# First MLP, blocks 8 to 17: normalisation and transposed parts issued ahead of the weight conversion steps

## The chip, the cores and the metric

The kernel runs on one core of a Trainium2 chip. The metric is the device time in microseconds of one execution. The kernel before was run three times: median 850.16 us, 850.09 to 852.99.

## The reference, cut to what matters

2304 tokens (4 batches of 576) of width 512 pass through three layers:

```python
x = attention(q, k, v, M_prev, z_prev, beta)   # 8 heads of 64, causal, with a memory term
h = x @ w_in                                   # first MLP, 512 -> 1024
e = exp(h - max(h)); solu = h * e / sum(e)
ln = (solu - mean(solu)) / sqrt(var(solu) + 1e-6) * g_ln
x = ln @ w_out                                 # 1024 -> 512
gate = sigmoid(x @ w_gate)                     # second MLP, 512 -> 1536
out = (gate * (x @ w_val)) @ w_out2            # 1536 -> 512
```

All weights come from DRAM as 64-bit floats.

## The kernel before, in words

**Layout.** The tokens are 18 blocks of 128 rows (t = 0 to 17). `X` stays on chip and holds the activations transposed. The attention runs first (lines up to 600), then the first MLP (`Moe1`), then the second (`Moe2`). The first MLP's blocks 0 to 7 overlap with the end of the attention and with the conversion of the first MLP's own weights; the change concerns the loop in `Moe1.run` over t = 8 to 17 and the entry into it, the branch for t = 8 (`t == NF1`). T1 is block 7. In the profiled execution the entry lies at about 266 us, the second MLP begins at about 431 us.

**One block of the first MLP.** Every product is done in three terms, since each operand is split into a high and a low part. The steps of block t, with their engines and lines:

- `h` (L658, TensorE): 48 matmuls into the PSUM tile `h`, which has two buffers.
- `max` (L671, VectorE), `exp` (L676, ACT, into the tile `e`), `mul` (L680 to L682, VectorE), `square` (L687 on ACT, then three tiny operations on GpSimd, L688 to L691, that yield scale and bias of the normalisation), `norm` (L695, ACT, in place on `e`).
- `trans` (L705, TensorE): eight transposes of `e` into two PSUM tiles `pl`, four each. There are two `pl` buffers in all, so the next block's transposes can write them only when this block's have been read by `parts(t, 0)` (L713, ACT: high parts into `lnT`) and by `parts(t, 1)` (L715, VectorE: low parts).
- three blocks form a group, and `product` (L724, TensorE) multiplies a group's `lnT` by the second weights into the PSUM tiles `po` (two buffers; po_0 to po_3 are the four column blocks of the result). `result` (L734, ACT) copies a finished `po` into `X`. `pieces(t)` hands out a group's products in halves, three halves for each block.
- `xsplit` (L644 ACT, L646 VectorE or GpSimd) splits the input of block t + 2 into the tile `xs`.

`ahead(t, n)` issues the first half of block t's `h` matmuls, then the transposes of block n, then the second half. So TensorE, which runs its instructions in order, waits in the middle of `h(t)` whenever the transposes of block t - 2 can't start.

**Weight conversion.** Beside this the loop converts the weights of the second MLP for its first six chunks (`Moe2.convert`, f = 0 to 5; `EARLY` is 6; the other six chunks are converted within the second MLP). A chunk is 15 steps: five each for w_val, w_gate and w_out. Of five steps, the first takes the exponent (L108, VectorE) and shifts it (L118, ACT), the second takes the mantissa (L111, VectorE), the third the sign (L121, VectorE, needs L118), the fourth the low word (L125, VectorE), and the fifth multiplies (L947, GpSimd). Among them stand sums of weight parts (L961, GpSimd, on the tile `M`), high parts `hi` (L969, ACT) and low parts `lo` (L975, VectorE, in place on `M`; for some parts GpSimd), and for w_out `hi_o` (L988, ACT, into the tile `ho`) and `lo_o` (L994, GpSimd). SP's queue saves the results to DRAM (L981, L982, L997) and loads the next raw weights (L105, into two buffers `raw`). Six end steps of a chunk are merged into the first six steps of the next chunk:

```python
chunk[4].append(loads[n][2])            # w_out of this chunk
chunk[9].append(loads[n + 1][0])        # w_val of the next
chunk[14].append(loads[n + 1][1])       # w_gate of the next
for x, y in zip(chunk, ends[n - 1]):
    x += y
```

**What sets the order.** Every engine runs its instructions in the order in which the program issues them, so the order in which `run` calls these functions is the schedule. `go(n)` issues the next n conversion steps. For t = 9 to 16 the order is: go(3); ahead(t, t - 2); high parts of t - 2; norm(t - 1); max(t); exp(t); go(2); low parts of t - 2; xsplit, mul(t), xsplit; square(t); three times a piece of products and go(1); then the steps left for this block. By the end of blocks 8 to 17 there are 24, 33, 41, 50, 58, 67, 75, 84, 93 and 96 steps issued.

## Time and profile before

| | |
|---|---|
| median of 3 runs | 850.16 us |
| profiled execution | 850.23 us, of which the span of the trace 848.4 us |
| mean granted TensorE clock | 0.994 |
| TensorE matmul (PE) busy | 831.8 us, 98% |
| TensorE weight load (PEld) busy | 734.2 us, 87% |
| VectorE (DVE) busy | 630.5 us, 74% |
| ACT busy | 467.9 us, 55% |
| GpSimd (POOL) busy | 481.0 us, 57% |

A share is busy time over the span, averaged over stages with different limits. A busy TensorE is not one at full speed: the granted clock tells that. The timeline shows one engine's instructions by start and duration, and behind a row the time for which the engine had stood idle and the instruction that released it. What an idle stretch costs is read from the engine that sets the pace of its stage.

### The profile page before, as it was taken

How to read it: one execution, taken by the hardware profiler on the slowest of the kernel's cores; microseconds unless marked ns; L12 is line 12 of the kernel's file. 1: busy time of each engine (PE TensorE's matmuls, PEld its weight loads, DVE VectorE, ACT ScalarE, POOL GpSimd, SP SyncE). 2: the span in 40 equal slices, each digit the busy share in tenths (PEclk: the TensorE clock that was granted, in tenths of full speed). 3: DMA queues.
4: the chain of work that ended last, by engine and by line, in shares of the span. 5: the costliest groups of instructions: out<-in, count | busy, mean ns of one | idle time of the engine just before them, and what ended most of it. 6: DMA issues, size and time to landing. Idle time of an engine off the chain costs nothing.

```text
span 848.4 us, 14831 instructions
## 1 busy us (share of the span) xinstructions
PE 831.8 (98%) x5020; PEld 734.2 (87%) x5020; DVE 630.5 (74%) x1379; ACT 467.9 (55%) x995; POOL 481.0 (57%) x579
## 2 busy tenths in 40 slices
PE   7999999999999999899999999999999999999998
PEld 5777777777788989799999999899999999999996
DVE  6899999997898687796447778878766445746645
ACT  5899999996697466676433345344533223424221
POOL 4787778774565667685406856876555242442111
PEclk9899999999999999999999999999999999999999
DMA  6544444430222455563278849993998773391662
GB/s 135 128 104 98 123 103 115 102 89 21 84 78 76 137 194 173 188 195 126 81 287 323 251 182 322 405 330 114 328 406 291 249 217 93 119 379 37 248 235 100
DMA packets 134971, 154.08 MB, mean 182 GB/s; under 512 B 69744, under 2 KB 103792, under 8 KB 134896
## 3 DMA queue, kind: packets, MB, share of 16 engines
q1 hardware_dynamic: 134576, 153.07, 55.5%
q8 instruction: 40, 0.66, 0.3%
q14 instruction: 35, 0.29, 0.1%
q10 hardware_dynamic: 320, 0.07, 0.0%
HBM read 116.92 MB, written 36.18 MB: 180 GB/s over the span
## 4 chain that ended last, share of the span: by engine, by line
PE 75%; DVE 9%; ACT 5%; DMA 4%; POOL 4%; issue 2%; SPq 0%; ACTq 0%; POOLq 0%; DVEq 0%
PE s L1114 16%; PE acc L1167 16%; PE g L1114 8%; PE po L724 7%; PE x L492 5%; PE sc L383 4%; PE v L1114 4%; PE h L658 3%; PE x L477 2%; PE sc L374 2%; DVE e L682 1%; PE trf L293 1%; DVE consts L671 1%; PE trk L293 1%; DMA raw<-in_moe_w_val_dram 1%
## 5 line engine op out<-in xcount | busy, mean ns | idle before, releaser
L1167 PE MATMUL acc<-o,G 128*128 128x512 f32 x648 | 181.6, 390 | 0.2 <-DVE G L1133 0.2
L1152 POOL TENSOR_TENSOR vl<-vl,sg 128x384 f32<-128x384 f32 x36 | 37.0, 1028 | 206.2 <-ACT sg L1151 206.2
L1167 PEld LDWEIGHTS acc<-o,G 128*128 128x128 f32 x648 | 118.6, 188 | 10.2 <-DVE G L1133 0.7
L422 POOL TENSOR_SCALAR p<-p,first,cols 128x256 f32<-128x256 f32 (+3 forms) x142 | 97.8, 703 | 6.3 <-DVE first L416 4.3
L411 ACT ACTIVATE p<-p,nm 128x128 f32<-128x128 f32 (+2 forms) x144 | 83.7, 595 | 2.0 <-DVE nm L405 0.8
L658 PE MATMUL h<-wih,xs 128*128 128x512 f32 x288 | 84.7, 400 | 0.0
L1144 ACT ACTIVATE sg<-sg 128x384 f32<-128x384 f32 x36 | 18.9, 526 | 104.1 <-DVE sg L1143 104.0
L724 PE MATMUL po<-lnT,woh 128*128 128x384 f32 x288 | 73.3, 335 | 0.0
L1133 DVE TENSOR_TENSOR G<-vl,G 128x384 fp32r<-128x384 f32 x72 | 54.4, 756 | 21.4 <-ACT G L1130 21.3
L1130 ACT CAST G<-vl 128x384 fp32r<-128x384 f32 x72 | 37.1, 515 | 45.2 <-POOL vl L1152 36.4
L658 PEld LDWEIGHTS h<-wih,xs 128*128 128x128 f32 x288 | 52.7, 190 | 10.5 <-POOL xs L646 0.7
L1151 ACT ACTIVATE sg<-sg 128x384 f32<-128x384 f32 x36 | 19.0, 526 | 75.2 <-DVE sg L1150 75.1
L405 DVE CUSTOM_DVE_ANT_0 p<-sc,mask 128x128 f32<-128x128 f32 (+3 forms) x128 | 54.9, 484 | 2.4 <-PE sc L383 1.4
L118 ACT ACTIVATE ex<-ex,consts 128x512 int32<-128x512 int32 (+1 forms) x52 | 34.7, 667 | 34.0 <-DVE ex L108 34.0
L724 PEld LDWEIGHTS po<-lnT,woh 128*128 128x128 f32 x288 | 52.0, 188 | 0.3
L947 POOL TENSOR_TENSOR M<-ex 128x256 f32<-128x256 f32 x48 | 42.6, 908 | 13.8 <-DVE ex L125 13.8
L724 PE MATMUL po<-lnT,wol 128*128 128x384 f32 x144 | 48.2, 335 | 0.0
L1138 DVE TENSOR_TENSOR u<-s,p 128x384 f32<-128x384 f32 x36 | 20.0, 556 | 36.0 <-PE s L1114 35.9
L333 POOL TENSOR_TENSOR G<-E,zm 128x640 f32<-128x640 f32 x16 | 25.0, 1563 | 37.7 <-DVE E L330 32.5
L121 DVE SCALAR_TENSOR_TENSOR ex<-raw,ex 128x512 int32<-128x512 int32 (+1 forms) x52 | 39.9, 767 | 7.7 <-ACT ex L118 7.6
L658 PE MATMUL h<-wil,xs 128*128 128x512 f32 x144 | 45.1, 394 | 0.0
L961 POOL TENSOR_TENSOR M<-M 128x256 f32<-128x256 f32 x48 | 42.2, 889 | 1.3
(710 smaller groups left out, 2442.6 us busy)
## 6 DMA issues: line engine op xcount, KB each, us to landing
o<-scro SPq DMA_DIRECT2D x36, 512.0 KB, 4.3
scrg<-hi SPq DMA_DIRECT2D x36, 256.0 KB, 4.6
scrg<-M SPq DMA_DIRECT2D x36, 256.0 KB, 4.6
raw<-in_moe_w_val_dram SPq DMA_DIRECT2D x12, 512.0 KB, 5.8
raw<-in_moe_w_gate_dram SPq DMA_DIRECT2D x12, 512.0 KB, 4.4
raw<-in_moe_w_out_dram SPq DMA_DIRECT2D x12, 512.0 KB, 5.1
scro<-ho SPq DMA_DIRECT2D x12, 512.0 KB, 2.8
out_dram<-X SPq DMA_DIRECT2D x18, 256.0 KB, 2.0
```

Source lines behind the costliest of these rows:

```text
L121: nc.vector.scalar_tensor_tensor(ex, raw[:, :, 1], -0x80000000, ex, ALU.bitwise_and, ALU.bitwise_or)
L405: nc.vector.tensor_tensor_reduce(p, x, m, -1.0, 3.0e38, ALU.add, ALU.min, nm)
L411: nc.scalar.activation(p, p, AF.Exp, bias=nm, scale=-1.0, accum_out=self.sum[n % 2][:, c, 0:1])
L422: eng.tensor_scalar(p, p, r["rs"][:, c : c + 1], og, ALU.mult, ALU.mult)
L492: nc.tensor.matmul(r["x", g][64 * hh : 64 * hh + 64, c0 : c0 + src.shape[1]], r["vt"][:, c : c + D], src, start=False, stop=j == 0,)
L658: lambda s=s, w=w, j=j: nc.tensor.matmul(ph[:, j * 512 : j * 512 + 512], xs[:, s, c], self.wi[c][w][:, j * 512 : j * 512 + 512], start=(c ...
L724: nc.tensor.matmul(self.po[g, m], w[:, m * P : m * P + P], L[x][c // 4][:, c % 4], start=(c == 0 and n == 0), stop=(c == NF1 - 1 and n == 2),)
L947: nc.gpsimd.tensor_mul(out[:, sl], m[:, sl], e[:, sl])
L961: ops[i][0](*ops[i][1:])
L1114: nc.tensor.matmul(po, W[:, a, c * P : c * P + P], xb[b][:, c], start=c + i == 0, stop=c == 1 and i == 2)
L1133: nc.vector.tensor_sub(G[:, 1, hs[h]], vl[:, h], f32(G[:, 0, hs[h]]))
L1167: nc.tensor.matmul(po, G[:, x, sl], o[:, w], start=first and i == 0, stop=stop and i == 2)
```

## The change

The body of the loop becomes a list of letters, `STEADY`, that is read for t = 8 to 17: m is `max`, e `exp`, g with a number so many conversion steps and g alone all that are left for this block, r the low parts of t - 2, x0 and x1 the two halves of `xsplit`, u `mul`, s `square`, p the next piece of products, n `norm(t)`, a `ahead(t + 1, t - 1)`, and q0 the high parts of t - 1. So `norm(t)` stands behind the pieces of block t, where before it stood in block t + 1 behind `go(3)` and the high parts; the transposes of t - 1 and their high parts follow within block t, ahead of the rest of its conversion steps; and the `go(3)` ahead of every block's maximum is gone. The steps that stood there come later, so that fewer steps have been issued when a block's maximum comes (58 and not 61 before that of block 13), but as many by the end of a block.

In the branch for t = 8, products and copies of block 7's pieces come first, with no step between the first two pieces, and `norm(T1)` follows the third; the transposes and both parts of block 6 follow at once.

In `convert`, for the six chunks of the first MLP, `lo(0, 2)` moves from the chunk's last step to the second end step, two steps later, and the two DMAs of `save(0, 2)` from the first end step to the third, behind `save_o`. The second MLP's own conversion (f from 6) keeps the old places.

```diff
@@ -25,6 +25,9 @@
 g1_c:0 n23_r:0 lz:2 s2_m:1 s3_p:1 g0_p:0 ph_s:1 s1_e:1 g0_c:0 s3_m:1 tt_p:0 n3_p:0 n2_p:0 cv_d:1 tf_p:1 t3_p:0
 tt_c:0 n01_r:1 cv_h:0 tc_p:0 tc_c:0 cv_l:0 tf_c:1 s4_p:1 t0_p:0 s4_m:1 ph_e:2
 """.split()
+
+
+STEADY = "m e g2 r x0 u x1 s g1 p g1 p g1 p n g1 a q0 g"


 COPY = dict(tc="v", tt="s", kh="s", x0="v", x1="v", g0="s", g1="v", t0="s", t1="s", t2="s", t3="s")
@@ -827,34 +830,46 @@
                 later += conv[done:n]
                 done = n
                 if t == NF1:
-                    go(3)
-                    self.norm(T1)
-                    for f, copy in self.pieces(T1):
+                    for i, (f, copy) in enumerate(self.pieces(T1)):
                         f(), copy and copy()
-                        go(2)
+                        if i == 2:
+                            self.norm(T1)
+                        go(0 if i == 0 else 3)
                     for x in range(2):
                         self.trans(t - 2, x)
-                else:
-                    if t < NBLK - 1:
-                        go(3)
-                    ahead(t, t - 2)
-                self.parts(t - 2, 0)
-                if t > NF1:
-                    self.norm(t - 1)
-                self.max(t)
-                self.exp(t)
-                go(2 if t < NBLK - 1 else 0)
-                self.parts(t - 2, 1)
-                if t + 2 < NBLK:
-                    self.xsplit(t + 2, 0)
-                self.mul(t)
-                if t + 2 < NBLK:
-                    self.xsplit(t + 2, 1)
-                self.square(t)
-                for f, copy in self.pieces(t):
-                    f(), copy and copy()
-                    go(1)
-                go(len(later))
+                    for x in range(2):
+                        self.parts(t - 2, x)
+                    assert t == NF1
+                todo = self.pieces(t)
+                for x in STEADY.split():
+                    if x[0] == "g":
+                        go(int(x[1:]) if x[1:] else len(later))
+                    elif x == "p":
+                        for f, copy in todo[:1]:
+                            f(), copy and copy()
+                        del todo[:1]
+                    elif x in ("x0", "x1"):
+                        if t + 2 < NBLK:
+                            self.xsplit(t + 2, int(x[1]))
+                    elif x == "m":
+                        self.max(t)
+                    elif x == "e":
+                        self.exp(t)
+                    elif x == "u":
+                        self.mul(t)
+                    elif x == "s":
+                        self.square(t)
+                    elif x == "r":
+                        if t > NF1:
+                            self.parts(t - 2, 1)
+                    elif t + 1 == NBLK:
+                        pass
+                    elif x == "n":
+                        self.norm(t)
+                    elif x == "a":
+                        ahead(t + 1, t - 1)
+                    else:
+                        self.parts(t - 1, int(x[1]))

         def pieces(self, t):

@@ -1007,10 +1022,12 @@
                 [v[0]], [v[1]], [v[2]], [v[3]], [new_m, v[4]],
                 [g[0]], [g[1], lambda: sums(0)], [g[2]], [g[3]], [g[4]],
                 [o[0], lambda: sums(1, 2)], [o[1], lambda: sums(3)], [o[2], lambda: hi(0, 2)], [o[3], lambda: hi(2, 4)],
-                [lambda: lo(0, 2), o[4], lambda: hi(4, 6)],
+                [*([] if f < EARLY else [lambda: lo(0, 2)]), o[4], lambda: hi(4, 6)],
             ]
             return loads, steps, [
-                [lambda: hi(6, 7), hi_o, lambda: save(0, 2)], [lo_o], [lambda: lo(4, 6, nc.gpsimd), save_o],
+                [lambda: hi(6, 7), hi_o, *([] if f < EARLY else [lambda: save(0, 2)])],
+                [lo_o, *([lambda: lo(0, 2)] if f < EARLY else [])],
+                [lambda: lo(4, 6, nc.gpsimd), save_o, *([lambda: save(0, 2)] if f < EARLY else [])],
                 [lambda: lo(6, 7, nc.gpsimd), lambda: save(4, 6)], [lambda: lo(2, 4), lambda: save(6, 7)], [lambda: save(2, 4)],
             ]
```

The order of TensorE's instructions is the same in both kernels. That of VectorE, ACT and GpSimd changes, and SP's in six places, one for each chunk. In the following rows a name with a number is a tile and its instance; line numbers of the changed kernel are higher by 3, behind `run` by 15.

**ACT, block 8 (the branch for t = 8).** `h_4012<-e_4111` is the square of block 7, `e_4111<-e_4111` its normalisation, `X<-po_...` the copies of the first three results, `ex` a conversion step. Before:

```order
L687 ACTIVATE h_4012,consts<-e_4111,consts 128x1024
L118 ACTIVATE ex_4146<-ex_4146,consts 128x512
L695 ACTIVATE e_4111<-e_4111,consts 128x1024
L734 COPY X<-po_0_3904 128x6x64
L734 COPY X<-po_1_3905 128x6x64
L118 ACTIVATE ex_4166<-ex_4166,consts 128x512
L734 COPY X<-po_2_4169 128x6x64
```

Now:

```order
L690 ACTIVATE h_4012,consts<-e_4111,consts 128x1024
L737 COPY X<-po_0_3904 128x6x64
L737 COPY X<-po_1_3905 128x6x64
L121 ACTIVATE ex_4154<-ex_4154,consts 128x512
L698 ACTIVATE e_4111<-e_4111,consts 128x1024
L737 COPY X<-po_2_4158 128x6x64
```

The copies of po_0 and po_1 stand directly behind the square; a conversion step and the normalisation come behind them.

**ACT, from the square of block 12 to its normalisation.** `h_4728<-e_4767` (now `h_4704<-e_4752`) is the square, `e_4767<-e_4767` (now `e_4752<-e_4752`) the normalisation of block 12, `lnT<-pl` the high parts of block 11, `hi`, `ho` and `ex` are conversion. Before:

```order
L687 ACTIVATE h_4728,consts<-e_4767,consts 128x1024
L734 COPY X<-po_1_4696 128x6x64
L118 ACTIVATE ex_4813<-ex_4813,consts 128x512
L734 COPY X<-po_2_4800 128x6x64
L969 CAST hi_4834<-M_4713 128x512 x3
L118 ACTIVATE ex_4844<-ex_4844,consts 128x512
L969 CAST hi_4834<-M_4713 128x256
L988 CAST ho_4848<-ex_4813 128x512
L713 CAST lnT_4608<-pl_0_4865 128x4x128
L713 CAST lnT_4608<-pl_1_4870 128x4x128
L695 ACTIVATE e_4767<-e_4767,consts 128x1024
```

Now:

```order
L690 ACTIVATE h_4704,consts<-e_4752,consts 128x1024
L737 COPY X<-po_1_4686 128x6x64
L737 COPY X<-po_2_4795 128x6x64
L698 ACTIVATE e_4752<-e_4752,consts 128x1024
L716 CAST lnT_4592<-pl_0_4840 128x4x128
L716 CAST lnT_4592<-pl_1_4845 128x4x128
L121 ACTIVATE ex_4864<-ex_4864,consts 128x512
L984 CAST hi_4872<-M_4754 128x512
L679 ACTIVATE e_4875,consts<-h_4827,consts 128x1024
```

The normalisation follows the copy of po_2, and behind it the high parts of block 11; the conversion instructions that stood between come elsewhere.

**VectorE, the same place.** `xs` is the input of block 14, `consts<-h` the maximum of block 13, `lnT<-pl` the low parts of block 11, `M<-M,hi` the low part of a weight, the other rows are conversion steps. Before:

```order
L646 TENSOR_TENSOR xs_4773<-X,xs_4773 128x2x4x64
L108 TENSOR_SCALAR ex_4813<-raw_4716 128x512
L111 TENSOR_SCALAR ex_4813<-raw_4716 128x512
L121 SCALAR_TENSOR_TENSOR ex_4813<-raw_4716,ex_4813 128x512
L125 SCALAR_TENSOR_TENSOR ex_4813<-raw_4716,ex_4813 128x512
L975 TENSOR_TENSOR M_4713<-M_4713,hi_4834 128x512
L108 TENSOR_SCALAR ex_4844<-raw_4798 128x512
L671 TENSOR_REDUCE consts<-h_4852 128x1
L111 TENSOR_SCALAR ex_4844<-raw_4798 128x512
L121 SCALAR_TENSOR_TENSOR ex_4844<-raw_4798,ex_4844 128x512
L715 TENSOR_TENSOR lnT_4608<-pl_0_4865,lnT_4608 128x4x128
L715 TENSOR_TENSOR lnT_4608<-pl_1_4870,lnT_4608 128x4x128
```

Now:

```order
L649 TENSOR_TENSOR xs_4769<-X,xs_4769 128x2x4x64
L114 TENSOR_SCALAR ex_4762<-raw_4665 128x512
L124 SCALAR_TENSOR_TENSOR ex_4762<-raw_4665,ex_4762 128x512
L128 SCALAR_TENSOR_TENSOR ex_4762<-raw_4665,ex_4762 128x512
L111 TENSOR_SCALAR ex_4864<-raw_4757 128x512
L114 TENSOR_SCALAR ex_4864<-raw_4757 128x512
L124 SCALAR_TENSOR_TENSOR ex_4864<-raw_4757,ex_4864 128x512
L674 TENSOR_REDUCE consts<-h_4827 128x1
L128 SCALAR_TENSOR_TENSOR ex_4864<-raw_4757,ex_4864 128x512
L718 TENSOR_TENSOR lnT_4592<-pl_0_4840,lnT_4592 128x4x128
L718 TENSOR_TENSOR lnT_4592<-pl_1_4845,lnT_4592 128x4x128
```

`M<-M,hi` no longer stands there, and one L108 less; one L125 (now L128) more stands behind the maximum.

**SP, the saves of chunk 0.** `scrg` and `scro` are the DRAM copies of the parts, `raw` the loads. Before:

```order
L105 DMA raw_4261<-in_moe_w_gate_dram 128x4x256
L981 DMA scrg_3602<-hi_4237 128x2x256
L982 DMA scrg_3602<-M_4161 128x2x256
L997 DMA scro_3603<-ho_4267 128x1024
L981 DMA scrg_3602<-hi_4237 128x2x256
L982 DMA scrg_3602<-M_4161 128x2x256
L105 DMA raw_4336<-in_moe_w_out_dram 128x1024
```

Now:

```order
L108 DMA raw_4262<-in_moe_w_gate_dram 128x4x256
L1012 DMA scro_3603<-ho_4268 128x1024
L996 DMA scrg_3602<-hi_4237 128x2x256
L997 DMA scrg_3602<-M_4174 128x2x256
L996 DMA scrg_3602<-hi_4237 128x2x256
L997 DMA scrg_3602<-M_4174 128x2x256
L108 DMA raw_4337<-in_moe_w_out_dram 128x1024
```

The two saves of `save(0, 2)` stand behind that of `ho` and no longer ahead of it; the two of `save(4, 6)` and the w_out load follow as before.

## Rows read from the trace of the kernel before

**Rows 1.** The page, part 1: busy us, share of the span, instructions.

```profile
PE 831.8 (98%) x5020; PEld 734.2 (87%) x5020; DVE 630.5 (74%) x1379; ACT 467.9 (55%) x995; POOL 481.0 (57%) x579
```

**Rows 2.** Windows: bounds, length, busy us (count) of each engine, PEclk, DMA share, GB/s.

```profile
431.00:848.40 417.40, 412.46 (x2161) 383.69 (x2159) 275.90 (x451) 145.77 (x273) 193.38 (x194) 1.00 0.71 248
...
272.00:431.00 159.00, 154.24 (x841) 143.70 (x842) 110.00 (x169) 91.95 (x160) 97.88 (x128) 0.99 0.47 153
```

**Rows 3.** Timeline of PE: start, duration, instruction, [idle before <-releaser], three marked gaps.

```profile
272.82 1.33 PE L724 MATMUL po<-lnT,wo 128*128 128x384 f32 x6 [1.45 <-ACT X L734]
...
315.38 1.22 PE L705 MATMUL pl<-ident,e 128*128 128x128 f32 x8 [0.85 <-DVE lnT L715]
...
354.68 1.97 PE L705 MATMUL pl<-ident,e 128*128 128x128 f32 x8 [3.08 <-ACT e L695]
```

**Rows 4.** Timeline of PE: first halves of blocks 11 to 15.

```profile
311.60 0.63 PE L658 MATMUL h<-wih,xs 128*128 128x512 f32 x2
...
325.46 0.63 PE L658 MATMUL h<-wih,xs 128*128 128x512 f32 x2
...
338.11 0.63 PE L658 MATMUL h<-wih,xs 128*128 128x512 f32 x2
...
348.68 0.63 PE L658 MATMUL h<-wih,xs 128*128 128x512 f32 x2
...
366.25 0.63 PE L658 MATMUL h<-wih,xs 128*128 128x512 f32 x2
```

**Rows 5.** Windows: two microseconds behind the stall of block 12.

```profile
356.00:358.00 2.00, 2.00 (x8) 1.71 (x7) 1.97 (x5) 0.76 (x2) 0.00 (x0) 0.50 0.85 289
```

**Rows 6.** Timeline of ACT: block 8, normalisation and copies to X.

```profile
271.16 1.24 ACT L695 ACTIVATE e<-e,consts 128x1024 f32<-128x1024 f32 x1 [0.82 <-POOL consts L691]
272.31 0.84 ACT L734 COPY X<-po 128x384 f32<-128x384 f32 x2
```

**Rows 7.** Timeline of ACT: high parts of block 11, normalisation of block 12.

```profile
352.42 1.07 ACT L713 CAST lnT<-pl 128x512 fp32r<-128x512 f32 x2
353.38 1.25 ACT L695 ACTIVATE e<-e,consts 128x1024 f32<-128x1024 f32 x1
```

**Rows 8.** Timeline of POOL: last number for the normalisation of block 12.

```profile
344.97 0.77 POOL L691 TENSOR_SCALAR consts<-consts 128x1 f32<-128x1 f32 x1
```

**Rows 9.** Timeline of DVE: from xs of block 14 to lnT of block 11.

```profile
342.59 0.69 DVE L646 TENSOR_TENSOR xs<-X,xs 128x512 fp32r<-128x512 f32 x1
...
344.98 0.71 DVE L121 SCALAR_TENSOR_TENSOR ex<-raw,ex 128x512 int32<-128x512 int32 x1 [1.02 <-ACT ex L118]
...
349.00 0.69 DVE L975 TENSOR_TENSOR M<-M,hi 128x512 fp32r<-128x512 f32 x1 [2.71 <-POOL M L961]
...
350.50 1.21 DVE L671 TENSOR_REDUCE consts<-h 128x1 f32<-128x1024 f32 x1
...
353.04 1.29 DVE L715 TENSOR_TENSOR lnT<-pl,lnT 128x512 fp32r<-128x512 f32 x2 [0.29 <-ACT lnT L713]
```

**Rows 10.** All instructions on tile raw, 255 to 440 us: ns min/median/max, starts.

```profile
L108 DVE TENSOR_SCALAR ex<-raw x18: 414/476/968, 269.1 to 383.6; 128x512 int32<-128x512 int32 x18
L111 DVE TENSOR_SCALAR ex<-raw x18: 415/472/964, 269.4 to 384.3; 128x512 int32<-128x512 int32 x18
L121 DVE SCALAR_TENSOR_TENSOR ex<-raw,ex x18: 679/709/1174, 270.4 to 386.6; 128x512 int32<-128x512 int32 x18
L125 DVE SCALAR_TENSOR_TENSOR ex<-raw,ex x18: 676/684/1228, 271.0 to 387.2; 128x512 f32<-128x512 uint16 x18
```

**Rows 11.** Timeline of DVE: first w_out step ahead of block 9's maximum; lnT of block 8.

```profile
299.14 0.75 DVE L108 TENSOR_SCALAR ex<-raw 128x512 int32<-128x512 int32 x1 [3.03 <-DMA raw<-in_moe_w_out_dram]
...
314.56 1.27 DVE L715 TENSOR_TENSOR lnT<-pl,lnT 128x512 fp32r<-128x512 f32 x2
```

**Rows 12.** Timeline of SP: a save of chunk 0 and the w_out load behind it.

```profile
293.57 0.36 SPq L982 DMA_DIRECT2D scrg<-M  x1
294.02 0.45 SPq L105 DMA_DIRECT2D raw<-in_moe_w_out_dram  x1
```

## The prediction

> **What bounds the kernel now.** I read the busy shares first: TensorE is busy 98% of the span [rows 1]. So only its gaps, and time that it spends at a slow clock, can be won, and the windows say where they lie: from 272 to 431 us, where most of the change works, TensorE is busy 154.24 of 159 us; behind 431 us, in the second MLP, 412.46 of 417.4 [rows 2]. The order there is untouched, so what the first MLP gains should be handed on nearly whole.
>
> TensorE's timeline has three marked gaps in the stretch [rows 3]. po_2, a product of block 8, waits 1.45 us for ACT's copy of po_0 into X, until 272.82. The transposes of block 9 wait 0.85 us for a low part on VectorE, until 315.38. Those of block 12 wait 3.08 us, put down to ACT's normalisation, until 354.68.
>
> A gap is not the whole price. The first halves of blocks 11 to 15 start at the times in [rows 4]: 12 to 13 takes 12.65 us without a stall. 11 to 12 and 14 to 15 hold the same work, but take 13.86 and 17.57. So the wait of 0.85 us costs 13.86 - 12.65 = 1.21 us, and that of 3.08 us costs 17.57 - 12.65 = 4.92. The extra 1.8 us of the latter is the clock: the granted share is 0.50 in 356 to 358 us, the 1.2 GHz level, after TensorE had done nothing from 351.60 to 354.68 [rows 3, 5]. In all 1.45 + 1.21 + 4.92 = 7.58 us can be won here.
>
> **The change part by part.** No instruction is added or removed. TensorE's order stays; those of ACT, VectorE and GpSimd change, and six places of SP's queue.
>
> *Block 8 (the T1 branch).* Before, ACT runs a conversion step behind the square, waits 0.82 us for GpSimd's scale, normalises block 7 (271.16), and only then copies po_0 and po_1 out (272.31) [rows 6]. Now the copies stand right behind the square. What ends last is then po_0 itself, complete at the latest when TensorE stopped, at 272.82 - 1.45 = 271.37. One copy is half of 0.84 us: po_2 can start by 271.8, which wins 1.0 us; if po_0 was complete sooner (three products of po_1 stand behind it), up to 1.45. I take **-1.2 us**, near the middle. The normalisation comes later by two copies; nothing reads it before the transposes of block 7, which stand behind all of block 8's products.
>
> *Transposes of block 12.* Two locks hold them, not one. The timeline names the normalisation, but the transposes also write the two pl tiles that block 11's transposes filled, and these come free when VectorE has read them: its lnT pair starts at 353.04 and takes 1.29, to 354.33, only 0.35 us before the transposes [rows 3, 9].
>
> The first lock: GpSimd's last number for this normalisation was ready at 344.97 + 0.77 = 345.74 [rows 8]. ACT got to it at 353.38, behind six conversion instructions and the high parts [rows 7]. Now it follows the copy of po_2 directly: it can run from 345.8 to 347.0, over 4 us before TensorE wants it at 351.60.
>
> The second: behind the normalisation come the high parts of block 11 at once (1.07 us, so to 348.1; they stood at 352.42) [rows 7]. On VectorE the low part of the weights, which waited 2.71 us for GpSimd (it overwrites in place what GpSimd's sums still read), no longer stands ahead of the maximum [rows 9]. From the end of xs (342.59 + 0.69 = 343.28) up to lnT there are now two each of L111, L121 and L125, one L108 and the maximum. With the medians of [rows 10] and 1.21 for the maximum that is 5.42 us, with the 1.02 us wait for ACT that [rows 9] shows 6.4: lnT starts at 349.7 and frees the first pl at 350.4. With every one at its longest it is 8.9 + 1.0: the first pl is free at 353.8. TensorE wants it at 351.60, so between 0 and 2.2 us of the stall stay. I take 0.2, since the medians are likelier than seven longest ones in a row: **-4.7 us**.
>
> *Transposes of block 9.* lnT of block 8 began at 314.56. Between xs of block 9 and it VectorE has ten instructions before and ten after, of like durations, so this stretch doesn't shrink by itself. What shrinks is its start: the maximum of block 9 stood behind the first step on the w_out weights, which waited 3.03 us for its load until 299.14 [rows 11]. Now that step comes behind the maximum and behind lnT of block 7. The chain ends up to 3 us earlier, where 0.85 was short: **-1.2 us**. The bounds are 0 (the wait only moves behind lnT) and 1.21.
>
> *The low part and the saves of each chunk.* One VectorE subtraction goes two steps back in the list, its duration stays. With it two saves move behind the save of ho, and so come directly ahead of GpSimd's saves and the next chunk's w_out load in SP's queue. Issues follow each other there at 0.45 us (293.57, 294.02) [rows 12], so five loads may leave 2 x 0.45 = 0.9 us later. It is hidden by the maximum (1.21) and lnT (1.28), which now run ahead of the step that needs the load; without that cover it costs up to 0.9 us in each of five chunks.
>
> *The rest.* As many steps as leave the place ahead of the maximum now run elsewhere. In blocks 14 to 16 that may leave a low part late: by the smallest such wait in the trace 1.21 us, by blocks without one nothing. I put 0.5 in between.
>
> Sum: -1.2 - 4.7 - 1.2 + 0.5 = -6.6 us. The profiled execution took 850.23 us (span 848.4), the median is 850.16, so nothing is to be corrected: **843.6 us**.
>
> **A rule that speaks against it.** The w_out load was issued at 294.02, behind the saves, and VectorE stood until 299.14 for it [rows 11, 12]. The Trainium skill's page "DMA: Bandwidth & Descriptors", section "Rules for kernel authors", says to issue a DMA early and to wait for its semaphore late; by it a change that puts saves ahead of a load loses. The trace agrees with it at that load. What its mechanism would cost here is rival 2.
>
> **The rivals.**
> 1. *The second lock stays shut*, or the stall only moves. ACT's steps for VectorE now queue behind the normalisation and the high parts; if VectorE waits there for them, lnT is as late as before. Then the big stall gives only the 0.35 us between the locks: 850.2 - 1.2 - 1.2 - 0.35 = 847.5 us, and with block 9 unmended too 848.7. For it: VectorE's total work doesn't shrink, and its idle time is waits for others [rows 9, 11]. Against it: the longest of those, 2.71 and 3.03 us, are just the ones that move. In this case the change doesn't do what it says.
> 2. *Slower: the w_out load becomes the bound.* If GpSimd's low parts still come late, the load leaves 0.9 us later, while VectorE asks for it no later, and waits 3.03 + 0.9 us; the next maximum and lnT queue behind that. It decides when this is more than VectorE's lead at the next transposes; each then costs TensorE a stall like the one of 3.08 us, 4.92 with the clock. In three of five chunks: 850.2 - 7.1 + 14.8 = 857.9 us. For it: the load was late once already. Against it: that wait of 3.03 us cost TensorE 1.21 at most.
> 3. *No wait at all is left*: 850.2 - 7.58 = 842.6 us.
>
> **How the numbers follow.** Forecast, with rival 3 in it (842.4 to 845.9): 0.70. Rival 1 (846 to 850): 0.22. Rival 2: 0.08. A measurement of this kernel can tell about 0.5% from no change, 4.25 us, so faster means under 845.9 and slower over 854.4: 0.70, 0.22 and 0.08. The range is 842.4 to 848.4: below it nothing is left to win here, and above it I leave out rival 2 and the tail of rival 1. What the second lock may keep (2.0 us over the sum, 845.6) and the uncovered loads (5 x 0.9 = 4.5 over it, 848.1) lie inside.
>
> **What would show it.** Right: from block 8's products to the second MLP no wait of TensorE over 1 us for a normalisation or a copy, no granted share below 1, the copies of po_0 and po_1 ahead of the normalisation, and the second MLP starting some 6.6 us sooner and taking as long as before. Wrong: the transposes wait for lnT instead of e; VectorE waits over 3 us for w_out loads in several chunks; the second MLP takes longer by what the first one gave.

## The result and the profile after

The changed kernel takes 843.59 us, median of 4 runs (843.14 to 844.54); the kernel before 850.74 beside it. The ratio is 0.9913, interval 0.9891 to 0.9934. Timed again in a later series, it gave 0.9925 (0.9906 to 0.9944). The profiled execution took 843.14 us.

The page, its span and part 1, against [rows 1], and the windows from 272 us to the first product of the second MLP and behind it, against [rows 2]:

```profile
span 841.3 us, 14834 instructions
...
PE 827.1 (98%) x5020; PEld 730.4 (87%) x5020; DVE 626.8 (74%) x1379; ACT 469.3 (56%) x995; POOL 482.7 (57%) x579
```

```profile
272.00:423.25 151.25, 150.47 (x832) 140.54 (x831) 108.09 (x171) 92.27 (x158) 98.98 (x128) 1.00 0.48 161
423.25:841.30 418.05, 412.38 (x2161) 383.81 (x2160) 274.67 (x451) 145.95 (x273) 194.07 (x194) 1.00 0.70 248
```

TensorE is now busy 150.47 of 151.25 us in the first window. The granted clock there is 1.00.

TensorE's timeline of the kernel before at three marks (the start of block 8's `h`, the transposes of block 6, which stand behind block 7's products, and the first product of the second MLP):

```profile
256.25 0.63 PE L658 MATMUL h<-wih,xs 128*128 128x512 f32 x2
...
281.28 1.03 PE L705 MATMUL pl<-ident,e 128*128 128x128 f32 x8
...
430.91 0.33 PE L1114 MATMUL g<-xb11h,gv0g 128*128 128x384 f32 x1
```

The same marks after, with the transposes that answer to [rows 3], and the first halves of blocks 14 and 15 that answer to [rows 4]:

```profile
255.03 0.63 PE L661 MATMUL h<-wih,xs 128*128 128x512 f32 x2
...
278.65 1.03 PE L708 MATMUL pl<-ident,e 128*128 128x128 f32 x8
...
312.68 1.23 PE L708 MATMUL pl<-ident,e 128*128 128x128 f32 x8 [0.78 <-DVE lnT L718]
...
345.95 0.63 PE L661 MATMUL h<-wih,xs 128*128 128x512 f32 x2
...
348.72 1.03 PE L708 MATMUL pl<-ident,e 128*128 128x128 f32 x8
...
358.59 0.63 PE L661 MATMUL h<-wih,xs 128*128 128x512 f32 x2
...
423.25 0.33 PE L1131 MATMUL g<-xb11h,gv0g 128*128 128x384 f32 x1
...
436.10 0.45 PE L1131 MATMUL g<-xb21h,gv1g 128*128 128x384 f32 x1 [1.17 <-DVE u L1155]
```

The wait of po_2 is gone, that of block 12's transposes too (348.72, no bracket, 1.03 us and not 1.97). That of block 9's transposes is still there, 0.78 us. A longer wait stands in the second MLP, 1.17 us at a product of its second chunk (`g<-xb21h,gv1g`) where before there were 0.27. It is the eleventh product there; the expectations below count wrongly and call it the sixth.

The difference of the marks from kernel to kernel tells where the 7.1 us of the two spans (848.4 - 841.3) come from:

| stretch | before - after at its end | gained in it |
|---|---|---|
| attention, to block 8 | 256.25 - 255.03 = 1.22 | 1.22 |
| block 8 | 281.28 - 278.65 = 2.63 | 1.41 |
| to block 14, with block 9's transposes | 348.68 - 345.95 = 2.73 | 0.10 |
| block 14, with block 12's transposes | 366.25 - 358.59 = 7.66 | 4.93 |
| to the second MLP | 430.91 - 423.25 = 7.66 | 0.00 |
| second MLP | 848.4 - 841.3 = 7.1 | -0.56 |

The 1.22 us of the attention aren't the change's. In the fourteen profiles of this text, all with the same attention, block 8 starts between 254.68 and 257.09 us. The second MLP, where its order is the same, takes 417.2 to 419.7 us. So spans are compared below by **the first MLP's stretch**, from the first product of block 8 to the first of the second MLP: 430.91 - 256.25 = 174.66 us before, 423.25 - 255.03 = 168.22 after, and 168.22 again in the repetition. That is 6.44 us less. Each stretch is read from one profile; where the first MLP is the same it repeats closely: 168.22 twice for the change, 167.08 to 167.10 in e7, e9 and e12.

ACT after, answering to [rows 6] and [rows 7], and VectorE ahead of the transposes of blocks 9 and 12 (there from xs of block 14), answering to [rows 11] and [rows 9]:

```profile
269.67 1.00 ACT L737 COPY X<-po 128x384 f32<-128x384 f32 x2 [1.59 <-PE po L727]
...
271.19 1.24 ACT L698 ACTIVATE e<-e,consts 128x1024 f32<-128x1024 f32 x1
...
339.36 1.25 ACT L698 ACTIVATE e<-e,consts 128x1024 f32<-128x1024 f32 x1 [0.93 <-POOL consts L694]
```

```profile
306.56 0.43 DVE L111 TENSOR_SCALAR ex<-raw 128x512 int32<-128x512 int32 x1 [2.17 <-DMA raw<-in_moe_w_val_dram]
...
308.93 1.21 DVE L674 TENSOR_REDUCE consts<-h 128x1 f32<-128x1024 f32 x1
...
311.86 1.28 DVE L718 TENSOR_TENSOR lnT<-pl,lnT 128x512 fp32r<-128x512 f32 x2
...
336.33 0.69 DVE L649 TENSOR_TENSOR xs<-X,xs 128x512 fp32r<-128x512 f32 x1
...
340.23 0.77 DVE L111 TENSOR_SCALAR ex<-raw 128x512 int32<-128x512 int32 x1 [1.68 <-DMA raw<-in_moe_w_out_dram]
...
342.95 1.21 DVE L674 TENSOR_REDUCE consts<-h 128x1 f32<-128x1024 f32 x1
...
344.91 1.27 DVE L718 TENSOR_TENSOR lnT<-pl,lnT 128x512 fp32r<-128x512 f32 x2
```

The normalisation of block 12 runs at 339.36, 9 us ahead of the transposes that read it. The low parts of block 11 (344.91) are 3.8 us ahead of them. The low parts of block 8 (311.86) are late as before, since VectorE now waits 2.17 us for the next chunk's w_val load.

### The profile page after: what moved, and what is told of

Its sections match the earlier page's. It is cut to its first block, busy times and chain, and to the rows that moved or that the text cites. A ratio compares the mean times of both kernels' runs of the same rounds, so it can differ in the third digit from the quotient of the medians.

```text
span 841.3 us, 14834 instructions
## 1 busy us (share of the span) xinstructions
PE 827.1 (98%) x5020; PEld 730.4 (87%) x5020; DVE 626.8 (74%) x1379; ACT 469.3 (56%) x995; POOL 482.7 (57%) x579
## 4 chain that ended last, share of the span: by engine, by line
PE 90%; DVE 4%; DMA 2%; ACT 1%; POOL 1%; issue 1%; SPq 0%; DVEq 0%; POOLq 0%
PE s L1131 17%; PE acc L1184 17%; PE h L661 10%; PE po L727 9%; PE g L1131 8%; PE x L495 5%; PE sc L386 4%; PE v L1131 4%; PE x L480 2%; DMA raw<-in_moe_w_val_dram 2%; PE pl L708 2%; PE sc L377 2%; PE trk L296 1%; PE trf L296 1%; PE trq L296 1%
## 5 line engine op out<-in xcount | busy, mean ns | idle before, releaser
L727 PE MATMUL po<-lnT,woh 128*128 128x384 f32 x288 | 73.4, 335 | 0.0
L727 PEld LDWEIGHTS po<-lnT,woh 128*128 128x128 f32 x288 | 52.1, 188 | 0.3
L727 PE MATMUL po<-lnT,wol 128*128 128x384 f32 x144 | 48.2, 335 | 0.0
```

The lines of the kernel that those rows point to most:

```text
L727: nc.tensor.matmul(self.po[g, m], w[:, m * P : m * P + P], L[x][c // 4][:, c % 4], start=(c == 0 and n == 0), stop=(c == NF1 - 1 and n == 2),)
```

## The experiments

Median and ratio are against the kernel before, timed beside each; the stretch is the first MLP's as above.

| run | median us | ratio, interval | stretch us |
|---|---|---|---|
| before | | | 174.66 |
| the change | 843.59 | 0.9913 (0.9891 to 0.9934) | 168.22 |
| e1 entry alone | 850.33 | 1.0001 (0.9986 to 1.0016) | 174.83 |
| e2 norm(t) ahead alone | 848.48 | 0.9982 (0.9971 to 0.9992) | 172.87 |
| e3 change, ACT late | 849.26 | 0.9991 (0.9975 to 1.0006) | 173.89 |
| e4 change, three steps back | 852.86 | 1.0028 (1.0010 to 1.0046) | 177.77 |
| e5 the change again | 844.77 | 0.9925 (0.9906 to 0.9944) | 168.22 |
| e6 change, old low part | 845.59 | 0.9933 (0.9912 to 0.9954) | 168.81 |
| e7 change, load first | 843.26 | 0.9903 (0.9882 to 0.9924) | 167.10 |
| e8 change, conversion loads first | 854.06 | 1.0034 (1.0020 to 1.0048) | 178.33 |
| e9 e7, conversion later | 849.77 | 0.9989 (0.9977 to 1.0001) | 167.09 |
| e10 change, norm(t) late | 846.35 | 0.9946 (0.9926 to 0.9965) | 169.76 |
| e11 change, high parts late | 844.04 | 0.9916 (0.9894 to 0.9937) | 169.09 |
| e12 e7, one step later | 842.83 | 0.9909 (0.9890 to 0.9928) | 167.08 |

**e1: the entry alone.** The branch for t = 8 as in the change, in the kernel before.

```diff
-                    go(3)
-                    self.norm(T1)
-                    for f, copy in self.pieces(T1):
+                    for i, (f, copy) in enumerate(self.pieces(T1)):
                         f(), copy and copy()
-                        go(2)
+                        if i == 2:
+                            self.norm(T1)
+                        go(0 if i == 0 else 3)
```

> The kernel before with the branch for t = 8 alone as in the change. Theory A (the wait of 1.45 us in block 8 was ACT's order alone, and TensorE hands on what it gains): po_2 no longer waits, the waits of 0.85 us (transposes of block 9) and 3.08 us (block 12) stay about as they were, 850.2 - 1.4 = 848.8 us. Rival (VectorE's chain ahead of the transposes of block 9 hangs on a load and not on TensorE): TensorE comes 1.4 us earlier to the same lock, the wait of 0.85 us grows to about 2.2 us, and the time stays at 850.2 us.

The wait of po_2 is gone, and the time is unchanged. TensorE's waits in the first MLP (total, times, longest):

```profile
PE pl L705 <- ACT e L695: 3.1, 1, 3.1
PE pl L705 <- DVE lnT L715: 1.4, 2, 0.9
```

The waits for lnT are now two, 0.47 us at the transposes of block 8 and 0.93 at those of block 9, with 0.35 us for a copy between them. The rival holds, in smaller pieces than it said: VectorE still waits 2.98 us for the w_out load until 299.39 (3.03 until 299.14 in [rows 11]), and TensorE, 1.4 us earlier, runs into what hangs on it. The entry's gain is kept only with the new order of the loop.

**e2: norm(t) behind the pieces, alone.**

```diff
                 self.parts(t - 2, 0)
-                if t > NF1:
-                    self.norm(t - 1)
...
                     f(), copy and copy()
                     go(1)
+                if t + 1 < NBLK:
+                    self.norm(t)
                 go(len(later))
```

> The kernel before with one move: norm(t) stands behind the pieces of block t, everything else in its old order. Theory A (two locks): the normalisation of block 12 is done before 348 us, but the low parts of block 11 on VectorE stay where they were, so the transposes of block 12 still wait 2.5 to 3 us, now put down to lnT; 0.35 us gained, 849.9 us. Rival C (the timeline's releaser is the whole cause): the wait is gone, 4.9 us gained with the clock, 845.3 us.

TensorE's and VectorE's timelines:

```profile
350.69 1.23 PE L705 MATMUL pl<-ident,e 128*128 128x128 f32 x8 [1.46 <-DVE lnT L715]
...
387.45 1.22 PE L705 MATMUL pl<-ident,e 128*128 128x128 f32 x8 [0.54 <-DVE lnT L715]
...
400.70 1.31 PE L724 MATMUL po<-lnT,wo 128*128 128x384 f32 x6 [0.90 <-ACT X L734]
```

```profile
345.82 0.69 DVE L975 TENSOR_TENSOR M<-M,hi 128x512 fp32r<-128x512 f32 x1 [2.72 <-POOL M L961]
...
349.86 1.29 DVE L715 TENSOR_TENSOR lnT<-pl,lnT 128x512 fp32r<-128x512 f32 x2 [0.28 <-ACT lnT L713]
```

The transposes of block 12 wait 1.46 us, for lnT and no longer for ACT: the second lock is there, as theory A said. Its size was wrong. VectorE's chain, low part with its 2.72 us for GpSimd included, happens to be 0.8 us further ahead of TensorE here (349.86 is 3.55 us behind the start of block 14's first half at 346.31; before, 353.04 - 348.68 = 4.36), and after this wait the granted clock stays at 1.00. So 3.1 us are gained there (14.47 and not 17.57 us from block 14's first half to block 15's), not 0.35 and not 4.9. The stretch is only 1.79 us shorter, and that is a sum: block 9's transposes no longer wait over 0.25 us, which gives 0.78 more, and 2.1 are lost behind block 15's first half, with the waits of 0.54 and 0.90 us.

**e3: ACT's moves taken back.** In the changed kernel:

```diff
-STEADY = "m e g2 r x0 u x1 s g1 p g1 p g1 p n g1 a q0 g"
+STEADY = "m e g2 r x0 u x1 s g1 p g1 p g1 p g1 a g q0 n"
```

> The changed kernel with ACT's moves taken back: the high parts of block t - 1 and then norm(t) stand behind all steps of the block, as in the kernel before; the steps keep their new places against the maximum. Theory A (ACT's two moves and VectorE's order are both needed): the transposes of block 12 wait 2 us or more for the normalisation or for lnT, 846 to 848 us. Rival B (what counts is which steps stand ahead of the maximum; ACT's moves are worth nothing): within 0.5 us of the changed kernel, 843.1 to 844.1 us, and no wait of TensorE over 1 us but the 0.8 us of block 9.

```profile
313.88 1.22 PE L708 MATMUL pl<-ident,e 128*128 128x128 f32 x8 [1.22 <-DVE lnT L718]
...
349.94 1.03 PE L708 MATMUL pl<-ident,e 128*128 128x128 f32 x8
...
386.67 1.23 PE L708 MATMUL pl<-ident,e 128*128 128x128 f32 x8 [0.72 <-DVE lnT L718]
...
401.21 1.52 PE L727 MATMUL po<-lnT,wo 128*128 128x384 f32 x6 [2.24 <-ACT X L737]
```

```profile
344.54 1.25 ACT L698 ACTIVATE e<-e,consts 128x1024 f32<-128x1024 f32 x1
```

```profile
403.00:405.00 2.00, 2.00 (x9) 1.90 (x8) 0.00 (x0) 0.00 (x0) 2.00 (x4) 0.50 0.84 277
```

Of the 6.44 us 5.67 are lost (173.89 - 168.22), and the median lies above the forecasts of both sides. But they are not lost where theory A put them: the transposes of block 12 (349.94) don't wait, those of blocks 9 and 15 wait 1.22 and 0.72 us, and a product behind block 17's `h` waits 2.24 us for a copy into X and TensorE falls to the 1.2 GHz level behind it (the window 403 to 405, PEclk 0.50). Behind the start of block 17's first half lie 429.67 - 383.02 = 46.65 us and not 423.25 - 381.79 = 41.46, so 5.19 of the 5.67. ACT's share is real, its place is the end. For block 12 it isn't needed: with VectorE's new order the normalisation runs at 344.54 from its old place, 5.4 us ahead of the transposes.

**e4: three steps ahead of the maximum again**, in the changed kernel:

```diff
+                if NF1 < t < NBLK - 1:
+                    go(3)
                 todo = self.pieces(t)
```

> The changed kernel with three steps put back ahead of the maximum of blocks 9 to 16; normalisation and high parts stay ahead of the rest of the steps, lo(0, 2) stays three steps later. Theory A (VectorE's order is the second lock): lnT comes late again in at least one block, its transposes wait 1 to 3 us for lnT, 844.5 to 848 us. Rival D (ACT's moves are the whole gain): within 0.5 us of the changed kernel, 843.1 to 844.1 us.

VectorE's and TensorE's timelines:

```profile
303.40 0.79 DVE L111 TENSOR_SCALAR ex<-raw 128x512 int32<-128x512 int32 x1 [3.67 <-DMA raw<-in_moe_w_out_dram]
304.11 1.21 DVE L674 TENSOR_REDUCE consts<-h 128x1 f32<-128x1024 f32 x1
```

```profile
307.00 1.22 PE L708 MATMUL pl<-ident,e 128*128 128x128 f32 x8 [3.59 <-DVE lnT L718]
...
356.45 1.22 PE L708 MATMUL pl<-ident,e 128*128 128x128 f32 x8 [1.69 <-DVE lnT L718]
```

Two microseconds behind the wait of 3.59 us, as a window:

```profile
308.00:310.00 2.00, 2.00 (x12) 1.68 (x10) 2.00 (x4) 0.93 (x1) 0.00 (x0) 1.00 0.03 8
```

9.55 us more in the stretch than the change, 3.1 more than before: the way that theory A said, and twice its price. The w_out step ahead of block 9's maximum waits 3.67 us for its load, the maximum and lnT come behind it, and TensorE stands 3.59 us. This is rival 2 of the prediction, at the point that it named: the load leaves late (298.58, 41.5 us behind block 8's start as in the change; before, 37.8) and VectorE asks for it no later. Further waits of 0.77 us at block 15's transposes and 1.76 for a copy follow. The expectation says that lo(0, 2) stays three steps later; by the diff it is two.

**e5: the change again.**

> The changed kernel itself, once more, as the measure for the other runs. Both theories: 843.6 us within 1 us; TensorE waits 0.8 us at the transposes of block 9 and 1.2 us at the sixth product of the second MLP, and nowhere else over 0.3 us from block 7 on. If its first part (the attention, which the change doesn't touch) takes 1 us more or less than in the first profile, the time moves by as much.

The median is 1.2 us higher than expected; in the profile the attention ends 1.5 us later (256.57 and 255.03). TensorE waits 0.75 us at block 9 and 0.61 in the second MLP, so that the latter's size moves from run to run.

**e6: lo(0, 2) and save(0, 2) in their old places**, in the changed kernel (the last hunk of the diff undone).

> The changed kernel with lo(0, 2) and save(0, 2) in their old places. Theory A: it matters where the old place stands directly ahead of a maximum, in block 15 (75 steps, five whole chunks): the low part waits up to 2.7 us for GpSimd there, lnT of block 13 is late by as much, less the lead that VectorE has: 0 to 2 us more, 843.6 to 845.6 us. Rival E (this part carries the change): the wait of 3 us at the transposes of block 12 or 14 comes back, 847 us or more. Rival F (it is worth nothing): no wait of TensorE moves by over 0.3 us.

0.59 us more in the stretch. VectorE's low part waits 2.88 us for GpSimd again, and a w_out step further on 1.77 us for its load:

```profile
367.06 0.69 DVE L990 TENSOR_TENSOR M<-M,hi 128x512 fp32r<-128x512 f32 x1 [2.88 <-POOL M L976]
...
383.20 0.87 DVE L111 TENSOR_SCALAR ex<-raw 128x512 int32<-128x512 int32 x1 [1.77 <-DMA raw<-in_moe_w_out_dram]
383.99 1.28 DVE L718 TENSOR_TENSOR lnT<-pl,lnT 128x512 fp32r<-128x512 f32 x2
```

TensorE at the transposes of blocks 9 and 15:

```profile
312.41 1.03 PE L708 MATMUL pl<-ident,e 128*128 128x128 f32 x8
...
384.81 1.22 PE L708 MATMUL pl<-ident,e 128*128 128x128 f32 x8 [0.56 <-DVE lnT L718]
```

The net time is of theory A's size, but its mechanism isn't shown. The wait of 2.88 us costs TensorE nothing there, since the transposes of block 14, which come behind it, don't wait. Those of block 15 wait 0.56 us for low parts that stand behind the w_out step, and a product waits 0.53 us for a copy. That load leaves about as late as in the change (122.7 and 122.4 us behind block 8's start), while TensorE comes 1.1 us sooner. The 0.59 us are a difference: from block 8's start to block 12's first half the run is 1.13 us shorter than the change, since block 9's transposes don't wait, and behind the start of block 17's first half it is 1.72 longer. So rival F is wrong too: the third part of the change costs the wait of block 9 and wins more at the end.

**e7: the w_out load ahead of the saves**, in the changed kernel, for f < EARLY:

```diff
...
+                    [lambda: hi(6, 7), hi_o], [lo_o, lambda: lo(0, 2)], [lambda: lo(4, 6, nc.gpsimd)],
+                    [lambda: lo(6, 7, nc.gpsimd)], [lambda: lo(2, 4), save_o, lambda: save(0, 2), lambda: save(4, 6)],
+                    [lambda: save(6, 7), lambda: save(2, 4)],
...
```

> The changed kernel with one change of SP's queue alone: for the first six chunks the w_out load stands ahead of the chunk's saves and not behind five of them. Theory G (the 0.78 us wait at the transposes of block 9 is VectorE's 2.17 us wait for the w_val load, late because it queues behind the saves and the w_out load): VectorE's waits for w_out loads (1.68 us in block 12, 1.57 us in block 15) go, that for the w_val load falls below 1 us, TensorE's wait at block 9 goes: 0.9 us less than the changed kernel, 842.7 us. Rival H (as many bytes go ahead of the w_val load as before, and it lands as late): the 0.78 us stay, 843.6 us.

SP's queue in the changed kernel (the save of ho, the w_out and the w_val load), and the same three here, where the load comes first:

```profile
293.56 0.34 SPq L1012 DMA_DIRECT2D scro<-ho  x1
...
296.55 0.55 SPq L108 DMA_DIRECT2D raw<-in_moe_w_out_dram  x1
...
299.39 0.55 SPq L108 DMA_DIRECT2D raw<-in_moe_w_val_dram  x1
```

```profile
292.09 0.34 SPq L108 DMA_DIRECT2D raw<-in_moe_w_out_dram  x1
294.21 0.34 SPq L1012 DMA_DIRECT2D scro<-ho  x1
...
299.61 0.45 SPq L108 DMA_DIRECT2D raw<-in_moe_w_val_dram  x1
```

Theory G holds. VectorE waits for no load between 270 and 400 us (2.17, 1.68 and 1.57 us in the changed kernel), TensorE waits nowhere in the first MLP, and the stretch is 1.12 us shorter. The w_val load leaves hardly sooner than in the changed kernel (299.61 and 299.39, which is 0.45 us sooner against block 8's start); it is the w_out load, 4.5 us earlier, that is out of its way. The whole time doesn't tell it apart from the change beside it (0.9903 and e5's 0.9925, intervals that overlap), and the profiled span is no shorter, since the second MLP takes 418.9 us.

**e8: the second MLP's first two raw loads ahead of its weight loads**, in the changed kernel.

```diff
-    m2.start()
     for x in first:
         x()
+    m2.start()
```

> The changed kernel with the second MLP's first two raw loads (w_val and w_gate of chunk 6) issued ahead of its first weight loads and not behind them. Theory I (the 1.17 us that TensorE waits at the sixth product of the second MLP is VectorE's first conversion step, which waits 1.82 us for that w_val load and stands ahead of the sum that frees TensorE's tile): the wait falls to 0.3 us or less, 0.9 us less than the changed kernel, 842.7 us. Rival J (the two loads hold up the first weight loads): the first product of the second MLP waits 1 us or more, 844.6 us or more.

SP's queue and TensorE:

```profile
425.00 0.37 SPq L108 DMA_DIRECT2D raw<-in_moe_w_val_dram  x1
...
426.52 0.43 SPq L1114 DMA_DIRECT2D gv0g<-scrg  x1
```

```profile
434.92 0.69 PE L1131 MATMUL g<-xb11h,gv0g 128*128 128x384 f32 x1 [9.95 <-DMA gv0g<-scrg]
```

Rival J, and far dearer than it said; the wait ends the stretch, which is 10 us longer. The two loads can leave only at 425.00, and the first weight load, which left at 399.66 in the changed kernel, stands behind them in the queue. The trace puts the last 17.1 us of SP's wait down to TensorE's `po` (L727), the last products of the first MLP; in the changed kernel the same w_val load left at 425.57. Against block 8's start that is 2.1 us sooner (168.4 and 170.5 us), and the weight load is 25 us later.

**e9: e7 with the conversion steps of the second MLP two places later.**

```diff
-            slots = [(i, j) for i in range(1, 3 * NA - 1) if i not in ends for j in range(6)]
+            slots = [(i, j) for i in range(1, 3 * NA - 1) if i not in ends for j in range(6)][2:]
```

> The changed kernel with the w_out load ahead of the chunk's saves (as in the run before of that name) and the second MLP's conversion steps two places later, so that the first of them no longer stands ahead of the sum that frees TensorE's tile. Theory I (TensorE's wait of 0.6 to 1.2 us at the sixth product of the second MLP is VectorE's wait for the w_val load): it falls to 0.3 us or less and the time to 842.5 us, 0.6 to 0.9 us under the version with the load first alone (843.3 us). Rival M (the load is as late for the next instruction and the wait only moves to a later product): 843.3 us.

The wait at `g<-xb21h,gv1g` is gone, as theory I said, but the time misses both forecasts by over 6 us: the second MLP takes 847.4 - 422.29 = 425.1 us, 6.2 more than in e7. TensorE's waits behind 440 us (in e7: 1.4 us for gv0s, 0.2 for u):

```profile
PE s L1135 <- DMA gv0s<-scrg: 3.0, 2, 1.7
PE s L1135 <- DVE u L1162: 2.8, 5, 0.8
PE s L1135 <- DVE sg L1164: 1.7, 2, 0.8
```

All other steps moved too, and TensorE now waits for `u` and `sg` on VectorE. Why it waits longer for the gv0s loads was not tried.

**e10 and e11: norm(t) alone, and the high parts alone, put back.**

```diff
-STEADY = "m e g2 r x0 u x1 s g1 p g1 p g1 p n g1 a q0 g"
+STEADY = "m e g2 r x0 u x1 s g1 p g1 p g1 p g1 a q0 g n"   # e10
+STEADY = "m e g2 r x0 u x1 s g1 p g1 p g1 p n g1 a g q0"   # e11
```

> The changed kernel with norm(t) alone put back behind all steps of the block; the high parts stay ahead of them. The run with both of ACT's moves taken back lost 4.5 us against the changed kernel. Theory K (it is the high parts: lnT on VectorE waits for them, and all that stands behind lnT): norm(t) alone costs under 1.5 us, 844 to 846 us, no wait of TensorE for a copy into X over 1 us. Rival L (it is the normalisation): 3 us or more, 847.5 us or more.

> The changed kernel with the high parts of block t - 1 alone put back behind all steps of the block; norm(t) stays ahead. Theory K (the high parts carry most of ACT's share): 3 us or more over the changed kernel, 847.5 us or more, with the wait of TensorE for the copy into X in the last blocks (2.24 us in the run with both moves taken back) there again. Rival L: under 1.5 us, 844 to 846 us.

Neither K nor L: norm(t) costs 169.76 - 168.22 = 1.54 us of stretch, the high parts 0.87, and both together 5.67 (e3). Either one ahead of the steps leaves the copies of the last blocks nearly in time (waits of 1.22 and 0.25 us); with both behind, the wait is 2.24 us and the clock falls.

**e12: e7 with only the first conversion step of the second MLP one place later.**

```diff
-                when.setdefault(slots[j * len(slots) // len(conv)], []).append(step)
+                when.setdefault(slots[max(1, j * len(slots) // len(conv))], []).append(step)
```

> The changed kernel with the w_out load ahead of the chunk's saves, and of the second MLP's conversion the first step alone one place later (behind the sum that frees TensorE's tile), all others where they were. Theory N (in the run that moved all steps by two places the wait at the sixth product did go, and the 7 us lost came from the other steps' new places): no wait of TensorE at the sixth product, none new over 1 us in the second MLP, 842.6 to 843.3 us. Rival O (the second MLP hangs on these places everywhere, the first one too): it loses 1 us or more against the version with the load first alone, 844.3 us or more.

Theory N: no wait at that product, none over 0.3 us behind 440 us, 840.7 - 423.66 = 417.0 us for the second MLP. The ratio's interval overlaps those of the change and of e7, so only the traces tell it apart: its stretch is 1.14 us shorter than the change's.

## Why the prediction came out

The time was forecast at 843.6 us and is 843.59, closer than the working deserves: block 9's term missed by 1.1 us and the rest by 0.5, the others made up for them by luck, and a profile's spread in parts that no one touched is larger.

- **Block 8: -1.2 forecast, -1.41 measured.** po_0 was complete 0.5 us before TensorE stopped: the copies now start at 269.67, where that stop would have come at 271.37 - 1.22 = 270.15, and nothing waits. The upper end of the bounds was right. e1 shows what the sum left out: alone this term is worth nothing, because VectorE's chain behind it doesn't come earlier with TensorE.
- **Block 12: -4.7 forecast, -4.93 measured.** Two locks were there, as argued: with the normalisation alone moved (e2) the wait turns from ACT to lnT; with the old number of steps ahead of the maximum and ACT's moves kept (e4) these transposes wait 1.69 us, for lnT. But one move opens both: with ACT's moves taken back and VectorE's order kept (e3) they don't wait, so moving the normalisation, the prediction's key to the first lock, isn't needed here. By the sum lnT would start 349.7 - 348.68 = 1.0 us behind the start of block 14's first half; it started 1.0 us ahead of it (344.91 and 345.95). The chain from xs took 344.91 - 337.02 = 7.9 us and not 6.4, of which 1.68 is a wait for a w_out load that the sum didn't have. But xs itself, taken as fixed, came 3.5 us sooner against TensorE (9.62 and 6.09 us ahead of that first half), which covered it.
- **Block 9: -1.2 forecast, 0.78 - 0.85 = -0.07 measured.** This is the term that failed, at the step "the chain ends up to 3 us earlier". The wait for the w_out load went, and one for the w_val load took its place: 2.17 us, until 306.56. The lower bound, that the wait only moves, was the right one. (The xs from which the prediction counts ten instructions is issued with block 9, but it is block 11's.) The prediction looked at the step that asks for the load and not at what the queue does with the load: the w_out load left at 296.55 and not 294.02, with TensorE 2.6 us ahead, and the w_val load landed behind it. e7 shows it: with the w_out load out of the way, the 0.78 us go. VectorE's start wasn't the only lever either: in e2 the old order of VectorE leaves no such wait, and of the 0.8 us by which its chain is sooner there, 0.49 is a wait for `exp` (L676), which ACT ran behind the normalisation before.
- **The saves: nothing, with up to 0.9 us a chunk if uncovered.** The loads did come later, by more than the sum had: the w_out load left 296.55 - 255.03 = 41.52 us behind block 8's start and not 294.02 - 256.25 = 37.77. VectorE waited for w_out loads (1.68 us in block 12, 1.57 in block 15) with leads that hid both. The w_val load behind them was not hidden: it is block 9's wait, which is gone with the saves and the low part in their old places (e6), so the term was too small. The cover named was the right one: e4 takes away the maximum of block 9 from ahead of the step, and TensorE pays 3.59 us.
- **The rest: +0.5 forecast, 0.00 measured** up to the second MLP. No low part is late; without the third part of the change (e6) 0.59 us are lost, 1.13 won and 1.72 lost.
- **The second MLP: handed on whole, by the forecast.** It took 0.56 us more, while the wait there grew by 1.17 - 0.27 = 0.90. Its scatter from run to run covers both.

So the change itself is worth 6.44 us of the first MLP's stretch against 6.6 forecast, and about 1 us of the profiled difference is the attention's scatter. Rival 1 was right in one of its two places. Rival 2's mechanism is real, and kept off by the lead that the change gives.

The rule weighed in the prediction (Trainium skill, "DMA: Bandwidth & Descriptors", "Rules for kernel authors": issue a DMA early, wait for it late) bears on e7, where the trace agrees: the load issued 4.5 us earlier ends VectorE's waits. e8 doesn't test it: there a load put far earlier in the program left only 2.1 us sooner against block 8's start, and the wait for the first weight load behind it cost TensorE 9.95 us.

## What to carry to other kernels

A transpose or product that waits for one engine may be held by a second that is only a little less late: work out when each lock opens, and test by opening one alone and by closing one alone. Here one move opened both. What a move gains on one engine is kept only if the next chain also comes earlier, so parts of a reordering aren't summed: here the entry alone gave 0, two halves of ACT's share cost 1.54 and 0.87 us but together 5.67. Before crediting the end of a wait for a load, follow the issuing queue: what stands ahead of it there, and which load comes behind.

## What was not expected of the hardware

- A TensorE gap's length alone doesn't tell whether the clock falls. It fell to the 1.2 GHz level behind gaps of 3.08 us ([rows 5]), 3.09 us (e1), 2.24 us (e3) and 9.95 us (e8, 0.50 from 435 to 439 us), and stayed at 1.00 behind 3.59 us (e4, the window 308 to 310) and 1.46 us (e2, windows 350 to 356). What differs was not tried.
- An instruction order that is the same to the last row in the attention still ends it between 254.68 and 257.09 us. A difference of 1 us in 850 is read from a stretch, not from a span.
